# Two decode layers on one core: the second form of the layers behind a branch as two nested loops, its watch tiles placed behind the load places, and the register load moved ahead of the last norm

## The chip, the cores and the metric

The kernel runs on one core of a Trainium2 chip. A core has five engines, each with an instruction stream of its own: TensorE (PE, matrix products; its weight loads are listed as PEld), VectorE (DVE), ScalarE (ACT), GpSimd (POOL) and SyncE (SP), which here starts nearly all DMA transfers. The engines wait for each other through semaphores. Data lies in HBM, in SBUF (128 partitions, addressed by byte within a partition) and in PSUM, where matrix products are summed. The metric is the device time of one execution in microseconds (us), lower is better.

## The reference

Two attention blocks and two MLP blocks in turn, for a batch of 8 with one new position each (x is 8 x 448). Attention has 16 query heads over 8 key-value heads of width 256 with a cache of 4096 positions; both attention blocks use the same cache and weights, and so do both MLP blocks.

```python
def _A_ref(x, k_cache, v_cache, wq, wo):
    q = (x @ wq) ...                                   # 8 x 16 heads x 256
    scores = einsum("bhqd,bhkd->bhqk", q, k) * (Dh ** -0.5)
    p = softmax(scores, axis=-1)
    o = einsum("bhqk,bhkd->bhqd", p, v)
    return o ... @ wo
def _B_ref(x, w1, w2, w3, w4):
    ...                                                # for one position hs is zero
    x1 = x + hs
    return x1 + gelu(layernorm(x1) @ w3) @ w4
x = x + _A_ref(layernorm(x), ...)
x = x + _B_ref(layernorm(x), ...)
x = x + _A_ref(layernorm(x), ...)
x = x + _B_ref(layernorm(x), ...)
```

The key and value caches are 8 x 8 x 4096 x 256 bf16 each, 134 MB each. The softmax of the reference takes off the largest score; a softmax without that gives the same numbers as long as the exponentials neither overflow nor vanish.

## The kernel before

The kernel holds the layers in two forms. The first, `layers_unshifted`, is the fast one: its softmax takes the exponential of the scores as they are. Beside the work it keeps a watch: `seen` gathers sums and reciprocals of the softmax denominators (POOL adds them at L574). Near the end (L1338 to L1343) PE and DVE boil `seen` down to one number, and DVE writes 0 or 1 into `bad`. The second form, `layers_shifted`, computes the same layers again with the maximum taken off, slowly. It runs only if `bad` is 1: every engine loads `bad` into a register (`values_load`, L39) and compares it at a branch (`tc.If`, L40). For the inputs of this case `bad` is 0, so the second form's instructions are not executed. They stand in each engine's program all the same, between the branch and the program's end. With the flag at 0 an engine runs a short else block, which brings its semaphores to the counts that the second form would have left, and then branches over the second form's instructions to the end (L1892 in the profile), where all engines meet at barriers. SP's else block waits first for the output transfers.

The fast form streams the caches. SBUF holds 17 places of 8 KB per partition in one tile, `places`; a K tile pair of 2 MB or a V chunk of 1 MB (in halves, 512 KB) lands in a place, is used, and the place is given to the next load. All loads are issued by SP in an order that a planner in the Python code writes out (`items`, `emit_loads`, `load_k` at L962, `load_v` at L976 and L979). K is transposed in place by DVE (L1054), PE makes the scores (L1069), ACT the exponentials (L1078), PE the products with V (L1137 and, for the last units, L1153). Some K and V chunks stay in SBUF or PSUM from the first attention block to the second. Projections, norms and MLP of each row run as generators, stepped between tiles. The scheduler of the framework is switched off for this part (`manual_schedule`): instructions stand in the order in which the code emits them.

After the last V chunk the last four rows are finished one operation after the other: DVE adds the attention's output to x (L1572), squares and sums (L1585, L1586, PE at L1588, DVE at L1590), centres (L1604), POOL takes the powers for the norm (L1614), PE multiplies with w3 (L1623), ACT applies gelu (L1656), PE multiplies with w4 (L1672), DVE adds (L1681), and SP and ACT send the output in two transfers each (L1683).

In SBUF the tiles are placed in the order of their pools. The pool `flags` with `seen` and `bad` is opened first, so these two lie at bytes 16512 and 16576, and `places` begins at byte 16608 of each partition.

The second form (`layers_shifted`, L1689 and on) is Python loops that are unrolled into the program: two layers, in each 8 rows x 8 key-value heads, and for each pair of row and head some 130 instructions on PE, 12 on DVE, two loads on SP. The register load in the profile's L39 stands where it is written, behind all of the fast form, though SP's was emitted ahead of its output transfers.

Of the kernel before, what the change touches and what calls it, by code (L numbers as in the profile page):

```python
# [8 lines left out]
FP32 = mybir.dt.float32  # L9
BF16 = mybir.dt.bfloat16  # L10
U32 = mybir.dt.uint32
ACT = mybir.ActivationFunctionType
ALU = mybir.AluOpType
# [5 lines left out]
def kernel(  # L19
# [15 lines left out]
    flags = ctx.enter_context(tc.tile_pool(name="flags", bufs=1))  # L35
    seen = flags.tile([128, 12], FP32, name="seen")
    bad = flags.tile([128, 1], mybir.dt.int32, name="bad")
    layers_unshifted(tc, seen[:], bad[:], A_x, A_k_cache, A_v_cache, A_wq, A_wo, B_x, B_w1, B_w2, B_w3, B_w4, out)
    flag = tc.nc.values_load(bad[0:1, 0:1], min_val=0, max_val=1)  # L39
# [5 lines left out]
def layers_unshifted(  # L45
    ctx: ExitStack,
    tc: tile.TileContext,
    seen: bass.AP,
    bad: bass.AP,
# [71 lines left out]

    nc.gpsimd.memset(seen, 0.0)
# [1443 lines left out]
    while gens:  # L1566
        step(10 * len(items))

# [113 lines left out]
    for q in range(4):  # L1682
        (nc.scalar if q % 2 else nc.sync).dma_start(  # L1683
            out[:, 0, W * q : W * q + W], xo[32 * q : 32 * q + Bn]
        )


@with_exitstack
def layers_shifted(  # L1689
# [44 lines left out]
    OT = keep.tile([128, Hq, 2, Bn], BF16, name="OT_s")  # L1734
# [38 lines left out]
    for _ in range(2):  # L1773
# [6 lines left out]
        for b in range(Bn):  # L1780
            for g in range(G):
                kt = work.tile([128, NS, Dh], BF16, name="kt")
                nc.sync.dma_start(kt[:], A_k_cache[b, g].rearrange("(p n) d -> p n d", p=128))
                vt = work.tile([128, NS, Dh], BF16, name="vt")
                nc.sync.dma_start(vt[:], A_v_cache[b, g].rearrange("(p n) d -> p n d", p=128))
                q_ps = psum.tile([128, 2, Dh], FP32, name="q_ps")
                nc.tensor.matmul(
                    q_ps[:].rearrange("p h d -> p (h d)"),
                    identb[:Bn, b : b + 1].to_broadcast([Bn, 128]),
                    q[:, 2 * Dh * g : 2 * Dh * (g + 1)],  # L1790
# [3 lines left out]
                q_all = work.tile([128, 2, Dh], FP32, name="q_all")  # L1794
                nc.vector.tensor_scalar_mul(q_all[:], q_ps[:], float(Dh) ** -0.5)
                s = work.tile([128, 2, NS], FP32, name="s")
                top = work.tile([128, 2], FP32, name="top")
                for h in range(2):
                    prod = work.tile([128, NS, Dh], FP32, name="prod")
                    nc.vector.tensor_tensor(  # L1800
                        prod[:],
                        kt[:],
                        q_all[:, h].unsqueeze(1).to_broadcast([128, NS, Dh]),
                        ALU.mult,
                    )
                    nc.vector.tensor_reduce(s[:, h], prod[:], mybir.AxisListType.X, ALU.add)
                nc.vector.tensor_reduce(top[:], s[:], mybir.AxisListType.X, ALU.max)
                top_ps = psum.tile([2, 128], FP32, name="top_ps")
                nc.tensor.matmul(top_ps[:], top[:], ident[:], start=True, stop=True)
                most = work.tile([2, 1], FP32, name="most")  # L1810
                nc.vector.tensor_reduce(most[:], top_ps[:], mybir.AxisListType.X, ALU.max)
                all_ps = psum.tile([128, 2], FP32, name="all_ps")
                nc.tensor.matmul(
                    all_ps[:], most[:].to_broadcast([2, 128]), ident[:2, :2], start=True, stop=True
                )
                down = work.tile([128, 2], FP32, name="down")
                nc.vector.tensor_scalar_mul(down[:], all_ps[:], -1.0)
                p = work.tile([128, 2, NS], FP32, name="p")
                z = work.tile([128, 2], FP32, name="z")
                for h in range(2):  # L1820
                    nc.scalar.activation(
                        p[:, h],
                        s[:, h],
                        ACT.Exp,
                        bias=down[:, h : h + 1],
                        accum_out=z[:, h : h + 1],
                    )
                z_ps = psum.tile([128, 2], FP32, name="z_ps")
                nc.tensor.matmul(z_ps[:], ones[:], z[:], start=True, stop=True)
                rz = work.tile([128, 2], FP32, name="rz")  # L1830
                nc.vector.reciprocal(rz[:], z_ps[:])
                pb = work.tile([128, NS, 2], BF16, name="pb")
                for h in range(2):
                    nc.vector.tensor_scalar(
                        pb[:, :, h], p[:, h], rz[:, h : h + 1], 1.0, ALU.mult, ALU.mult
                    )
                o_ps = psum.tile([128, 2, 2], FP32, name="o_ps")
                for j in range(2):
                    for n in range(NS):
                        nc.tensor.matmul(  # L1840
# [56 lines left out]
```

## Time and profile before

| what | value |
|---|---|
| median of 3 runs | 1039.92 us (1039.06 to 1040.02) |
| the profiled execution | 1039.2 us |
| its span, first to last instruction | 1037.4 us |
| instructions executed | 28804 |
| PE / PEld busy | 660.3 / 417.4 us (64% / 40%) |
| DVE / ACT / POOL busy | 585.7 / 213.3 / 35.4 us (56% / 21% / 3%) |
| granted TensorE clock, mean | 0.639 |
| read from HBM | 419.63 MB, 405 GB/s over the span |

The profile is one execution, recorded by the hardware. Times are in us from the first instruction, durations of single instructions in ns. L12 is line 12 of the kernel before. An engine's name with a q (SPq, PEldq) is its instruction sequencer: register loads, branches, waits and DMA issues are its work and are not counted as busy. `x2: 43/46/49, 1031.5 to 1033.2` reads: two of these, shortest, median and longest duration, and the start of the first and of the last. A row by stretch gives the stretch and its length, then PE, PEld, DVE, ACT and POOL busy in us with the number of instructions, the granted clock, the busy share of the 16 DMA engines and GB/s. A row of DMA queues gives packets, MB and the time that the packets took as a share of 16 engines over the span; a queue of kind "instruction" carries the engines' programs. The chain that ended last is followed back from the last instruction, and its shares say in whose work the span went.

### The profile page before, as it was taken

The numbers are of one execution on the slowest core, as the hardware profiler recorded it, in microseconds if no ns is written. First come the engines' busy times: TensorE is split into PE (matmuls) and PEld (weight loads), VectorE is DVE, ScalarE is ACT, GpSimd is POOL, SyncE is SP. The second block draws the span as 40 slices with busy tenths as digits, with TensorE's granted clock in tenths as the row PEclk, the third lists the DMA queues.
The fourth block names the chain that finished last, engine by engine and source line by source line (L and its number), as shares of the span: only waits on it lengthen the run. The fifth ranks groups of instructions, "written<-read, shape, count | busy, mean of one in ns | idle before, by whom it ended". The sixth has DMA issues, their size and how long they took to land.

```text
span 1037.4 us, 28804 instructions
## 1 busy us (share of the span) xinstructions
PE 660.3 (64%) x12708; PEld 417.4 (40%) x12708; DVE 585.7 (56%) x1213; ACT 213.3 (21%) x689; POOL 35.4 (3%) x138
## 2 busy tenths in 40 slices
PE   2164445875587657765874687557765875686674
PEld 2032223553255334533552355334432453355454
DVE  6345576259616951695159615961696169625661
ACT  1010111141214121312141214121411141214110
POOL 0000000000000000000000000000000000000100
PEclk9999555576556556655566666565655566656555
DMA  9999999999999999999999999999999999999993
GB/s 381 410 425 420 420 423 415 399 423 423 412 400 425 425 409 391 414 424 411 402 417 425 411 403 420 424 412 392 424 422 406 402 417 423 411 392 414 419 419 148
DMA packets 68020, 421.58 MB, mean 406 GB/s; under 512 B 7080, under 2 KB 11952, under 8 KB 42288
## 3 DMA queue, kind: packets, MB, share of 16 engines
q1 hardware_dynamic: 67840, 419.66, 98.7%
q8 instruction: 101, 1.65, 0.6%
q14 instruction: 31, 0.25, 0.1%
q10 hardware_dynamic: 48, 0.01, 0.0%
HBM read 419.63 MB, written 0.01 MB: 405 GB/s over the span
## 4 chain that ended last, share of the span: by engine, by line
DMA 48%; DVE 24%; PE 20%; issue 4%; ACT 2%; SPq 1%; POOL 0%; DVEq 0%; ACTq 0%; POOLq 0%
DMA places<-in_A_v_cache_dram 36%; DVE places L1054 18%; DMA places<-in_A_k_cache_dram 11%; PE sc L1069 8%; PE o L1137 5%; PE misc L634 2%; PE misc L205 2%; DVE store L1100 2%; DVE qbd L449 1%; DMA w_sb<-in_B_w_dram 1%; PE misc L566 1%; SPq L224 1%; ACT p_n L1078 1%; PE misc L487 1%; DVE rz L569 1%
## 5 line engine op out<-in xcount | busy, mean ns | idle before, releaser
L1054 DVE STREAM_TRANSPOSE places<-places 128x512 uint32<-128x512 uint32 (+2 forms) x384 | 443.8, 1212 | 44.4 <-DMA places<-in_A_k_cache_dram 43.9
L1137 PE MATMUL o<-places,ptw 128*8 128x256 bf16 x3808 | 245.9, 382 | 139.6 <-DMA places<-in_A_v_cache_dram 110.5
L1069 PE MATMUL sc<-places,qbd 128*8 128x256 bf16 (+1 forms) x4736 | 237.1, 355 | 149.3 <-DVE places L1054 147.9
L1069 PEld LDWEIGHTS <-qbd 128*8 128x8 bf16 x4736 | 123.2, 104 | 218.6 <-DVE places L1054 125.3
L1137 PEld LDWEIGHTS <-ptw 128*8 128x8 bf16 x3968 | 102.5, 101 | 205.1 <-issue 127.4
L1078 ACT ACTIVATE p_n<-sc 128x256 bf16<-128x256 f32 x128 | 95.6, 747 | 329.4 <-PE sc L1069 326.8
L1319 ACT COPY ptw<-psv 128x32 bf16<-128x32 bf16 x248 | 52.7, 228 | 180.0 <-PE o L1137 178.4
L449 DVE CAST qbd<-misc 32x16 bf16<-32x16 f32 (+1 forms) x184 | 30.8, 167 | 63.6 <-PE misc L443 61.8
L634 PE MATMUL misc<-R_t,o_t 128*128 128x4 f32 (+1 forms) x212 | 45.6, 321 | 28.0 <-DVE qbd L449 11.6
L634 PEld LDWEIGHTS misc<-R_t,o_t 128*128 128x128 f32 x212 | 41.4, 272 | 44.4 <-issue 17.8
L569 DVE RECIPROCAL rz<-misc 128x4 f32<-128x4 f32 (+1 forms) x55 | 9.5, 172 | 84.9 <-PE misc L566 40.4
L1127 ACT CAST psv<-misc 128x128 bf16<-128x128 f32 x64 | 17.0, 266 | 195.7 <-PE misc L1120 195.7
L1105 ACT COPY places<-store 128x1024 bf16<-128x1024 bf16 x40 | 40.3, 1029 | 10.5 <-PE o L1137 10.1
L566 PE MATMUL misc<-zm,few 128*128 128x4 f32 (+1 forms) x110 | 28.6, 331 | 19.2 <-DVE zm L558 16.8
L574 POOL TENSOR_TENSOR seen<-seen,rz 128x4 f32<-128x4 f32 (+1 forms) x55 | 11.1, 202 | 842.2 <-DVE rz L569 813.1
L566 PEld LDWEIGHTS misc<-zm,few 128*128 128x128 f32 x110 | 23.8, 269 | 35.0 <-DVE zm L558 23.3
L1078 ACT ACTIVATION_READ_ACCUMULATOR p_n<-sc 128x1 f32 x128 | 34.1, 266 | 0.0
L205 PEld LDWEIGHTS <-w_sb 128*128 128x128 bf16 x896 | 27.4, 104 | 16.1 <-issue 16.1
L588 ACT COPY o_t<-o 128x256 f32<-128x256 f32 x53 | 19.8, 373 | 57.7 <-PE o L1137 57.7
L1100 DVE TENSOR_SCALAR store<-places 128x512 uint32<-128x512 uint32 x40 | 24.8, 674 | 0.0
L1120 PEld LDWEIGHTS <-p_n 128*128 128x128 bf16 x256 | 11.6, 105 | 29.9 <-issue 18.9
L638 DVE CAST qT<-misc 128x8 bf16<-128x8 f32 (+1 forms) x37 | 7.3, 196 | 27.9 <-PE misc L634 20.2
(165 smaller groups left out, 394.0 us busy)
## 6 DMA issues: line engine op xcount, KB each, us to landing
places<-in_A_k_cache_dram SPq DMA_DIRECT2D x79, 2048.0 KB, 15.3
places<-in_A_v_cache_dram SPq DMA_DIRECT2D x193, 512.0 KB, 7.1
places<-in_A_v_cache_dram SPq DMA_DIRECT2D x87, 1024.0 KB, 19.1
places<-in_A_k_cache_dram SPq DMA_DIRECT2D x34, 1024.0 KB, 11.8
rest<-in_A_v_cache_dram SPq DMA_DIRECT2D x8, 640.0 KB, 16.8
places<-in_A_wq_dram SPq DMA_DIRECT2D x5, 768.0 KB, 13.1
places<-in_A_v_cache_dram SPq DMA_DIRECT2D x8, 384.0 KB, 16.3
wo_sb<-in_A_wo_dram SPq DMA_DIRECT2D x1, 2688.0 KB, 19.0
```

Source lines behind the costliest of these rows:

```text
L205: nc.tensor.matmul(bass.AP(out.tensor, out.offset, [out.ap[0], (1, WIDE)]), w, x.to_broadcast([128, WIDE]), start=start, stop=stop, skip_g ...
L449: nc.vector.tensor_copy(qbd[32 * a : 32 * a + 32, :, g0 : g0 + ng, a, :], qs.rearrange("p e (f g u h) -> p (e f) u g h", f=2, u=2, h=2)[:, ...
L566: nc.tensor.matmul(z_ps, ones, zm[:], start=True, stop=True)
L569: nc.vector.reciprocal(rz[:], z_ps)
L634: nc.tensor.matmul(ot_ps[:, j], o_sb[:].rearrange("p (i j) -> p j i", j=2)[:, j], R, start=True, stop=True)
L1054: nc.vector.transpose(w, w)
L1069: nc.tensor.matmul(sc[32 * k : 32 * k + 8, 128 * (x % 2) : 128 * (x % 2 + nx)], qbd[:, ep, gp % 2].rearrange("p a h -> p (a h)"), v, start ...
L1078: nc.scalar.activation(p_sb[:, :, :, 2 * u : 2 * u + 2].rearrange("p t i x -> p x t i"), sc[:, 0:256].rearrange("p (x t i) -> p x t i", x= ...
L1100: nc.vector.tensor_single_scalar(kept_words.bitcast(U32), words.bitcast(U32), 0, op=ALU.bitwise_or)
L1105: nc.scalar.copy(words, kept_words.bitcast(BF16))
L1137: nc.tensor.matmul(o_ps[32 * q : 32 * q + 8, :], ptz[:, at : at + 8], v[:, y * Dh : (y + 1) * Dh] if v2 is None or y < PR else v2[:, (y - ...
L1319: nc.scalar.copy(ptw[:, ring_of[it], :, 6:8], psv[slot_of[it[0]]][:, it[2]])
```

## The change

Three things change. First, in the second form the loop over the two layers and the loop over the 64 pairs of row and head become loops of the engines (`tc.For_i`), so that each body stands in the program once. For that the second form is rewritten in part: queries go through a DRAM tile `q_rows` and are broadcast by a DMA, the loads take their row from the loop's register, probabilities stay unscaled in bf16 and the output is scaled, turned by PE, and stored at a register's offset. Second, `seen` and `bad` are no longer a pool of their own ahead of the others but tiles of the pool `consts`, asked for after the tile `places`; `places` then begins at byte 16512. Third, the register load of `bad` is moved from the outermost function into `layers_unshifted`, behind the last tile and ahead of the last norm, and its check of the loaded value against its bounds is left out. In the built program the fast form's instructions are otherwise the same, in the same order.

```diff
--- before.py
+++ after.py
@@ -32,11 +32,7 @@
     out: bass.AP,
 ):
 
-    flags = ctx.enter_context(tc.tile_pool(name="flags", bufs=1))
-    seen = flags.tile([128, 12], FP32, name="seen")
-    bad = flags.tile([128, 1], mybir.dt.int32, name="bad")
-    layers_unshifted(tc, seen[:], bad[:], A_x, A_k_cache, A_v_cache, A_wq, A_wo, B_x, B_w1, B_w2, B_w3, B_w4, out)
-    flag = tc.nc.values_load(bad[0:1, 0:1], min_val=0, max_val=1)
+    flag = layers_unshifted(tc, A_x, A_k_cache, A_v_cache, A_wq, A_wo, B_x, B_w1, B_w2, B_w3, B_w4, out)
     with tc.If(flag > 0, preferred_fallthrough_block=False):
         layers_shifted(tc, A_x, A_k_cache, A_v_cache, A_wq, A_wo, B_x, B_w1, B_w2, B_w3, B_w4, out)
 
@@ -45,8 +41,6 @@
 def layers_unshifted(
     ctx: ExitStack,
     tc: tile.TileContext,
-    seen: bass.AP,
-    bad: bass.AP,
     A_x: bass.AP,
     A_k_cache: bass.AP,
     A_v_cache: bass.AP,
@@ -119,6 +113,8 @@
         n_few[0] += n
         return few[:, at : at + n]
 
+    seen = consts.tile([128, 12], FP32, name="seen")[:]
+    bad = consts.tile([128, 1], mybir.dt.int32, name="bad")[:]
     nc.gpsimd.memset(seen, 0.0)
     usel = small(4)
     for u in range(2):
@@ -1565,6 +1561,12 @@
         step(idx, it in narrow)
     while gens:
         step(10 * len(items))
+    flag = nc.values_load(
+        bad[0:1, 0:1],
+        min_val=0,
+        max_val=1,
+        skip_runtime_bounds_check_because="a comparison writes 0 or 1",
+    )
 
 
     nb = Bn - MID
@@ -1683,6 +1685,7 @@
         (nc.scalar if q % 2 else nc.sync).dma_start(
             out[:, 0, W * q : W * q + W], xo[32 * q : 32 * q + Bn]
         )
+    return flag
 
 
 @with_exitstack
@@ -1731,7 +1734,11 @@
     nc.sync.dma_start(rows[:], A_x.rearrange("b s d -> (b s) d"))
     x = keep.tile([Bn, D], FP32, name="x_s")
     nc.vector.tensor_copy(x[:], rows[:])
-    OT = keep.tile([128, Hq, 2, Bn], BF16, name="OT_s")
+    OT = keep.tile([128, Bn * G, 2, 2], BF16, name="OT_s")
+    dram = ctx.enter_context(tc.tile_pool(name="q_rows", bufs=1, space=bass.MemoryType.DRAM))
+    q_rows = dram.tile([Bn * G, 2 * Dh], BF16, name="q_rows")
+    k_all = A_k_cache.rearrange("b g (p n) d -> (b g) p n d", p=128)
+    v_all = A_v_cache.rearrange("b g (p n) d -> (b g) p n d", p=128)
 
     def norm(dst, src):
         mean = work.tile([Bn, 1], FP32, name="mean")
@@ -1770,84 +1777,83 @@
             )
         return ps[:, 0:width]
 
-    for _ in range(2):
+    with tc.For_i(0, 2, 1):
         xn = work.tile([Bn, D], BF16, name="xn")
         norm(xn[:], x[:])
         xT = columns(xn, 112, KC, "xT_s")
         q = work.tile([Bn, HD], BF16, name="q_s")
         for at in range(0, HD, 512):
             nc.vector.tensor_copy(q[:, at : at + 512], times(xT, wq, KC, at, 512))
-        for b in range(Bn):
-            for g in range(G):
-                kt = work.tile([128, NS, Dh], BF16, name="kt")
-                nc.sync.dma_start(kt[:], A_k_cache[b, g].rearrange("(p n) d -> p n d", p=128))
-                vt = work.tile([128, NS, Dh], BF16, name="vt")
-                nc.sync.dma_start(vt[:], A_v_cache[b, g].rearrange("(p n) d -> p n d", p=128))
-                q_ps = psum.tile([128, 2, Dh], FP32, name="q_ps")
+        nc.sync.dma_start(q_rows[:].rearrange("(b g) c -> b (g c)", b=Bn), q[:])
+        with tc.For_i(0, Bn * G, 1) as i:
+            kt = work.tile([128, NS, Dh], BF16, name="kt")
+            nc.sync.dma_start(kt[:].unsqueeze(1), k_all[bass.ds(i, 1)].rearrange("o p n d -> p o n d"))
+            vt = work.tile([128, NS, Dh], BF16, name="vt")
+            nc.sync.dma_start(vt[:].unsqueeze(1), v_all[bass.ds(i, 1)].rearrange("o p n d -> p o n d"))
+            qb = work.tile([128, 2, Dh], BF16, name="qb")
+            nc.sync.dma_start(
+                qb[:].rearrange("p h d -> p (h d)"),
+                q_rows[bass.ds(i, 1), :].to_broadcast([128, 2 * Dh]),
+            )
+            q_all = work.tile([128, 2, Dh], FP32, name="q_all")
+            nc.vector.tensor_scalar_mul(q_all[:], qb[:], float(Dh) ** -0.5)
+            s = work.tile([128, 2, NS], FP32, name="s")
+            top = work.tile([128, 2], FP32, name="top")
+            for h in range(2):
+                prod = work.tile([128, NS, Dh], FP32, name="prod")
+                nc.vector.tensor_tensor(
+                    prod[:],
+                    kt[:],
+                    q_all[:, h].unsqueeze(1).to_broadcast([128, NS, Dh]),
+                    ALU.mult,
+                )
+                nc.vector.tensor_reduce(s[:, h], prod[:], mybir.AxisListType.X, ALU.add)
+            nc.vector.tensor_reduce(top[:], s[:], mybir.AxisListType.X, ALU.max)
+            top_ps = psum.tile([2, 128], FP32, name="top_ps")
+            nc.tensor.matmul(top_ps[:], top[:], ident[:], start=True, stop=True)
+            most = work.tile([2, 1], FP32, name="most")
+            nc.vector.tensor_reduce(most[:], top_ps[:], mybir.AxisListType.X, ALU.max)
+            all_ps = psum.tile([128, 2], FP32, name="all_ps")
+            nc.tensor.matmul(
+                all_ps[:], most[:].to_broadcast([2, 128]), ident[:2, :2], start=True, stop=True
+            )
+            down = work.tile([128, 2], FP32, name="down")
+            nc.vector.tensor_scalar_mul(down[:], all_ps[:], -1.0)
+            p = work.tile([128, NS, 2], BF16, name="p")
+            z = work.tile([128, 2], FP32, name="z")
+            for h in range(2):
+                nc.scalar.activation(
+                    p[:, :, h],
+                    s[:, h],
+                    ACT.Exp,
+                    bias=down[:, h : h + 1],
+                    accum_out=z[:, h : h + 1],
+                )
+            z_ps = psum.tile([2, 1], FP32, name="z_ps")
+            nc.tensor.matmul(z_ps[:], z[:], ones[:, 0:1], start=True, stop=True)
+            rz = work.tile([2, 1], FP32, name="rz")
+            nc.vector.reciprocal(rz[:], z_ps[:])
+            o_ps = psum.tile([2, Dh], FP32, name="o_ps")
+            for n in range(NS):
                 nc.tensor.matmul(
-                    q_ps[:].rearrange("p h d -> p (h d)"),
-                    identb[:Bn, b : b + 1].to_broadcast([Bn, 128]),
-                    q[:, 2 * Dh * g : 2 * Dh * (g + 1)],
+                    o_ps[:], p[:, n], vt[:, n], start=(n == 0), stop=(n == NS - 1)
+                )
+            o_row = work.tile([2, Dh], BF16, name="o_row")
+            nc.vector.tensor_scalar(o_row[:], o_ps[:], rz[:], 1.0, ALU.mult, ALU.mult)
+            turn = psum.tile([128, 2, 2], FP32, name="o_turn")
+            for j in range(2):
+                nc.tensor.matmul(
+                    turn[:, j],
+                    o_row[:, 128 * j : 128 * j + 128],
+                    identb[:2, :2],
                     start=True,
                     stop=True,
                 )
-                q_all = work.tile([128, 2, Dh], FP32, name="q_all")
-                nc.vector.tensor_scalar_mul(q_all[:], q_ps[:], float(Dh) ** -0.5)
-                s = work.tile([128, 2, NS], FP32, name="s")
-                top = work.tile([128, 2], FP32, name="top")
-                for h in range(2):
-                    prod = work.tile([128, NS, Dh], FP32, name="prod")
-                    nc.vector.tensor_tensor(
-                        prod[:],
-                        kt[:],
-                        q_all[:, h].unsqueeze(1).to_broadcast([128, NS, Dh]),
-                        ALU.mult,
-                    )
-                    nc.vector.tensor_reduce(s[:, h], prod[:], mybir.AxisListType.X, ALU.add)
-                nc.vector.tensor_reduce(top[:], s[:], mybir.AxisListType.X, ALU.max)
-                top_ps = psum.tile([2, 128], FP32, name="top_ps")
-                nc.tensor.matmul(top_ps[:], top[:], ident[:], start=True, stop=True)
-                most = work.tile([2, 1], FP32, name="most")
-                nc.vector.tensor_reduce(most[:], top_ps[:], mybir.AxisListType.X, ALU.max)
-                all_ps = psum.tile([128, 2], FP32, name="all_ps")
-                nc.tensor.matmul(
-                    all_ps[:], most[:].to_broadcast([2, 128]), ident[:2, :2], start=True, stop=True
-                )
-                down = work.tile([128, 2], FP32, name="down")
-                nc.vector.tensor_scalar_mul(down[:], all_ps[:], -1.0)
-                p = work.tile([128, 2, NS], FP32, name="p")
-                z = work.tile([128, 2], FP32, name="z")
-                for h in range(2):
-                    nc.scalar.activation(
-                        p[:, h],
-                        s[:, h],
-                        ACT.Exp,
-                        bias=down[:, h : h + 1],
-                        accum_out=z[:, h : h + 1],
-                    )
-                z_ps = psum.tile([128, 2], FP32, name="z_ps")
-                nc.tensor.matmul(z_ps[:], ones[:], z[:], start=True, stop=True)
-                rz = work.tile([128, 2], FP32, name="rz")
-                nc.vector.reciprocal(rz[:], z_ps[:])
-                pb = work.tile([128, NS, 2], BF16, name="pb")
-                for h in range(2):
-                    nc.vector.tensor_scalar(
-                        pb[:, :, h], p[:, h], rz[:, h : h + 1], 1.0, ALU.mult, ALU.mult
-                    )
-                o_ps = psum.tile([128, 2, 2], FP32, name="o_ps")
-                for j in range(2):
-                    for n in range(NS):
-                        nc.tensor.matmul(
-                            o_ps[:, j],
-                            vt[:, n, 128 * j : 128 * j + 128],
-                            pb[:, n],
-                            start=(n == 0),
-                            stop=(n == NS - 1),
-                        )
-                nc.vector.tensor_copy(
-                    OT[:, 2 * g : 2 * g + 2, :, b], o_ps[:].rearrange("p j h -> p h j")
-                )
-        o_cols = OT[:].rearrange("p h j b -> p (h j) b")
+            nc.vector.tensor_copy(
+                OT[:, bass.ds(i, 1)].rearrange("p o h j -> p (o h) j"),
+                turn[:].rearrange("p j h -> p h j"),
+            )
+        o_cols = OT[:].rearrange("p (b g) h j -> p (g h j) b", b=Bn)
         nc.vector.tensor_add(x[:], x[:], times(o_cols, wo, HD // 128, 0, D))
         n1 = work.tile([Bn, D], FP32, name="n1")
         norm(n1[:], x[:])
```

## Prediction

> **What bounds the kernel now.** I read the page first (DMA queues, chain that ended last), then busy time by stretch, then by line the instructions of the register load (L39), the branch (L40) and the program's end (L1892).
>
> From the page:
>
> ```profile
> q1 hardware_dynamic: 67840, 419.66, 98.7%
> q8 instruction: 101, 1.65, 0.6%
> q14 instruction: 31, 0.25, 0.1%
> ...
> DMA 48%; DVE 24%; PE 20%; issue 4%; ACT 2%; SPq 1%; POOL 0%; DVEq 0%; ACTq 0%; POOLq 0%
> ```
>
> The load queue is busy for 98.7% of the span, so until the last load lands nothing but the transfers counts. Queues 8 and 14 carry instructions: the engines fetch their programs while they run. Busy time by stretch:
>
> ```profile
> 1005.00:1023.00 18.00, 12.66 (x335) 11.04 (x336) 2.41 (x18) 2.67 (x6) 0.68 (x4) 0.50 0.88 357
> 1023.00:1037.40 14.40, 5.46 (x160) 4.59 (x159) 3.47 (x21) 0.53 (x3) 1.99 (x2) 0.50 0.03 7
> ```
>
> After 1023 us the DMA share is 0.03: the last 14.4 us are a serial tail, in which a microsecond is a microsecond. The output DMAs, the branch, and what stands behind it:
>
> ```profile
> L1683 SPq DMA_DIRECT2D out_dram<-places x2: 287/330/373, 1030.7 to 1031.1; - x2
> ```
>
> ```profile
> L40 POOLq COMPARE_BRANCH  x2: 38/42/45, 1027.8 to 1029.3; - x2
> L40 PEldq COMPARE_BRANCH  x2: 95/1836/3577, 1030.2 to 1030.6; - x2
> L40 DVEq COMPARE_BRANCH  x2: 51/53/55, 1031.1 to 1031.3; - x2
> L40 SPq COMPARE_BRANCH  x2: 43/46/49, 1031.5 to 1033.2; - x2
> L40 ACTq COMPARE_BRANCH  x2: 38/46/53, 1032.1 to 1032.2; - x2
> ```
>
> ```profile
> L1892 SPq EVENT_SEMAPHORE  x10: 17/28/28, 1036.1 to 1037.3; - x10
> ...
> L1892 POOLq DRAIN  x3: 34/41/82, 1029.4 to 1037.1; - x3
> ...
> L1892 PEldq DRAIN  x2: 8/40/73, 1034.2 to 1037.0; - x2
> L1892 DVEq DRAIN  x2: 10/34/57, 1034.2 to 1036.9; - x2
> L1892 ACTq DRAIN  x2: 8/38/67, 1034.9 to 1036.9; - x2
> ```
>
> Each engine branches twice: once on the flag, once from the short else block over the second form's code to the end. POOL needs 0.16 us for the second (branch 1029.29, next instruction 1029.45). The others need PE 3.6 us (1030.56 to 1034.20), DVE 2.9 (1031.29 to 1034.25), ACT 2.6 (1032.23 to 1034.87), SP 2.85 (1033.23 to 1036.08). In each such gap the trace's packet records have one instruction packet about 1.1 us after the branch (DVE 1032.35, ACT 1033.18, SP 1034.44 of 8192 B; PE 1031.66 of 16384 B), and a second some 0.6 us after the engine goes on. POOL has none. So a far jump costs a fetch of the target's page. SP is last: it branches only when the output has landed (its waits end at 1033.2), so its 2.85 us end the kernel.
>
> **The change, part by part.** *1. The second form becomes loops.* The data does not take the branch (its work is not in the trace), so only the size of the code jumped over matters. Counted in the two built programs, by engine, before and after: PE 17619 and 355 (364 with the second passes of three fp32 products), DVE 1910 and 126, SP 522 and 89, ACT 275 and 61, POOL 21 and 62. The fast path is the same instructions in the same order but for part 3, and the else block and the end have as many as before.
>
> Which pages does an engine hold? One instruction is 64 B, so a packet is 128 instructions, for PE 256; PE's 101 packets against its 25,520 executed instructions say one packet per page walked, and the pair after a jump (target, then next) says that page and next are held. Aligning packet times with instruction counts, SP stands about 54 into its page at the jump: 74 are left there and 128 in the next, and 89 lands 15 into the held next page. ACT: about 10 + 128 left, jump 61, held. DVE: about 12 + 128, jump 126, held by some 14, near the edge. POOL stays in its own. PE: about 79 + 256 = 335 left, jump 364: beyond.
>
> Sum: SP goes on at 1033.23 + 0.16 (POOL's row) = 1033.39 instead of 1036.08. Its eight waits and drain took 0.63 us (1036.08 to 1036.71): 1034.02. PE is late next: it still fetches, branches no earlier (its branch waits for its own last matmul), drains at 1034.20 with 0.07, and POOL's gathering then stands at about 1034.31 instead of 1036.71: **-2.40 us**. Were PE's page held, SP would end it: 1036.71 - 1034.02 = -2.69. DVE, if it fetches after all, comes at 1034.25, no later than PE. The ends: 0 (a target in the next page stalls like a far one, nearest row SP's 2.85) and -2.7. I take -2.4, since the page count puts three engines inside and PE outside.
>
> [...]
>
> *2. The watch's two tiles lie behind the places.* `places` starts at byte 16512 of each partition instead of 16608 (32 past a multiple of 64 before, 0 after). No instruction changes; the target addresses of about 51,000 packets of 4, 8 and 16 KB do, 3,190 per engine. Rows: 1792-byte packets take 74 ns at best, both into `wo_sb` (a multiple of 64) and into `places`; 4096-byte ones 159 ns mostly into `wq_sb` (aligned) and, early, into `places`. So alignment shows no price: 0. Ends: V's 8192-byte packets mostly take 313 ns but 309 when alone, K's 614 against 611, V's 4096 about half at 162 or more against 159. If the shift gave all that back, (15,488 x 4 + 10,112 x 3 + 12,700 x 3) / 16 engines = 8.1 us gained; I know no row against the mirror image, so +6.4 us (2 ns each) is the other end.
>
> *3. Register loads ahead of the last norm.* Each engine waits for `bad` (written 1022.79, 0.155 us), loads (0.479 to 0.562 us), and goes on.
>
> ```profile
> L39 SPq TENSOR_LOAD <-bad x1: 479/479/479, 1023.0 to 1023.0; - x1
> ...
> L39 POOLq TENSOR_LOAD <-bad x1: 498/498/498, 1027.2 to 1027.2; - x1
> L39 PEldq TENSOR_LOAD <-bad x1: 488/488/488, 1029.6 to 1029.6; - x1
> L39 DVEq TENSOR_LOAD <-bad x1: 545/545/545, 1030.5 to 1030.5; - x1
> L39 ACTq TENSOR_LOAD <-bad x1: 562/562/562, 1031.4 to 1031.4; - x1
> ```
>
> What is removed lies on no path that ends: DVE's, PE's and ACT's stood in front of branches whose engines come in before SP. What is added queues in front of the norm. DVE: behind L581 (ends 1024.17), ahead of L1572, which starts at 1024.81 when PE's L487 is done: 1024.17 + 0.545 + 0.07 = 1024.79, just hidden. PE: behind L487 (last ends 1024.77), ahead of L1588's wait for DVE (over at 1025.43): 1024.77 + 0.488 + 0.10 = 1025.36, hidden. ACT has nothing between 1022.6 and 1028.6, POOL nothing from 1018.5 to 1027.2. SP's load stays where it was; its range check (0.2 us at 1023.5) goes while SP waits for the output until 1030.7: 0. If DVE's cover failed, up to +0.6 us; in the queue order it could gain nothing. I take 0.
>
> *4. Two register moves on SP* ahead of the first barrier: 0.035 us each by POOL's move at 0.73; SP reaches that barrier 0.3 us before PE: 0.
>
> The profiled execution took 1039.2 us, span 1037.4, 1.8 outside. With -2.4 the span is 1035.0 and that execution 1036.8. The median of the runs is 1039.92, 0.7 above it; on the median: 1039.9 - 2.4 = **1037.5**.
>
> **Rivals.**
> *PE's target is held too.* For: only its two packets after the jump tell its depth, and 29 instructions decide. Against: the same two packets. SP ends it: 1037.2. [...]
> *The next page does not help.* A taken branch refetches unless it stays in its page, as POOL's did, the only short jump in the trace. SP then stalls 2.85 us as before: 1039.9. Against: the next page has been fetched long before (SP's last packet at 944.5).
> *The shift speeds the loads.* 1039.9 - 2.4 - 8.1 = 1029.4 at the full end, 1033.5 at half. Against: equal best times on both alignments. [...]
> *Slower: the shift slows the loads.* Same place, other sign: each nanosecond on 3,190 packets an engine is 3.2 us, so it eats the gain at 0.75 ns and is slower by 0.2% from 1.4 ns. At 2 ns: 1039.9 - 2.4 + 6.4 = 1043.9. For: the queue is full, nothing hides it. Against: the same best times.
>
> **How the numbers follow.** Forecast 0.45 (1037.5), PE held 0.20 (1037.2), no help from the next page 0.17 (1039.9), loads faster 0.10, loads slower 0.08. A measurement of this kernel can tell about 0.2% (2.1 us; the three runs span 1.0). The forecast clears that by 0.3 us, so three in four of it count as faster, nine in ten of the second case, all of the fourth: 0.34 + 0.18 + 0.10 = 0.62 faster; 0.30 within; 0.08 slower. The range leaves out the last two cases (0.18): from 1036.0 (second case, less 1.2 for run to run and the 1.8 us outside the span) to 1040.4 (third case plus 0.5). The first case alone: 1036.7 to 1038.3.
>
> **What would show it.** SP's first L1892 instruction within 0.3 us of its second branch; no instruction packet between; PE's second branch still about 3.6 us long and its drain the last to come in; DVE's L1572 and PE's L1588 no later after the last load; medians of 8192- and 16384-byte packets unchanged at 313 and 614 ns. It is wrong if SP still shows a gap near 2.9 us, if the 98.7% stretch ends at another time by over 1 us, or if L1572 waits for the load.

## The result, and the profile after

The changed kernel takes 1034.18 us (median of 6 runs, 1034.10 to 1035.51), the kernel before beside it 1040.08 us (6 runs, 1039.06 to 1041.33): a ratio of 0.9944, 95% interval 0.9931 to 0.9957. That is faster by 0.56%. The forecast was 1037.5 us with a range down to 1036.0: the sign was right, the size was not, and the time lies below the range.

The profiled execution took 1034.15 us, its span 1032.4 (before: 1039.2 and 1037.4). The rows that answer to those of before follow. From the page, the queues (packets, MB, share), what was read from HBM, and the chain:

```profile
q1 hardware_dynamic: 67840, 419.66, 99.0%
q8 instruction: 101, 1.65, 0.7%
q14 instruction: 28, 0.23, 0.1%
...
HBM read 419.63 MB, written 0.01 MB: 406 GB/s over the span
...
DMA 47%; DVE 26%; PE 18%; issue 4%; ACT 2%; SPq 1%; POOL 0%; DVEq 0%; ACTq 0%
```

The same packets and bytes, and still a queue that is full all the time. But the span is shorter, so the same packets took less time each. Three instruction packets are gone from queue 14 (31 to 28): the page fetches of SP, DVE and ACT behind the branch.

The first operation behind the last load (L1572 before, L1574 now), and busy time by stretch, as in the prediction:

```profile
L1572 DVE TENSOR_TENSOR xT<-xT,store x1: 172/172/172, 1024.8 to 1024.8; 128x16 f32<-128x16 f32 x1
L1574 DVE TENSOR_TENSOR xT<-xT,store x1: 171/171/171, 1021.3 to 1021.3; 128x16 f32<-128x16 f32 x1
```

```profile
1000.00:1019.40 19.40, 12.43 (x351) 11.05 (x340) 4.01 (x21) 3.05 (x7) 0.68 (x4) 0.66 0.90 371
1019.40:1032.40 13.00, 5.55 (x160) 4.68 (x160) 3.58 (x22) 0.53 (x3) 1.99 (x2) 0.50 0.03 6
```

This splits the gain in two. The add starts at 1021.30 us instead of 1024.81: **the stretch of the loads is 3.51 us shorter**. From there to the end it is 11.08 us instead of 12.60: **the tail is 1.52 us shorter**. Together 5.03 us of span. The prediction had 0 for the first and 2.40 for the second.

In the tail, the register loads, the output's issues, the branches and the end:

```profile
L1564 SPq TENSOR_LOAD <-bad x1: 478/478/478, 1019.6 to 1019.6; - x1
L1564 ACTq TENSOR_LOAD <-bad x1: 475/475/475, 1019.6 to 1019.6; - x1
...
L1564 DVEq TENSOR_LOAD <-bad x1: 541/541/541, 1020.4 to 1020.4; - x1
L1564 PEldq TENSOR_LOAD <-bad x1: 488/488/488, 1020.8 to 1020.8; - x1
```

```profile
L1685 SPq DMA_DIRECT2D out_dram<-places x2: 298/332/367, 1027.2 to 1027.6; - x2
```

```profile
L36 POOLq COMPARE_BRANCH  x2: 38/42/45, 1023.7 to 1025.8; - x2
L36 PEldq COMPARE_BRANCH  x2: 95/1984/3872, 1026.1 to 1027.0; - x2
L36 DVEq COMPARE_BRANCH  x2: 51/53/55, 1026.9 to 1027.3; - x2
L36 SPq COMPARE_BRANCH  x2: 43/46/49, 1028.0 to 1030.6; - x2
L36 ACTq COMPARE_BRANCH  x2: 38/44/49, 1028.1 to 1028.3; - x2
```

```profile
L1898 SPq EVENT_SEMAPHORE  x10: 17/28/28, 1031.1 to 1032.3; - x10
...
L1898 DVEq DRAIN  x2: 10/34/57, 1027.9 to 1031.9; - x2
L1898 ACTq DRAIN  x2: 8/44/79, 1028.7 to 1031.9; - x2
L1898 PEldq DRAIN  x2: 8/40/73, 1031.0 to 1032.0; - x2
```

SP branches the second time at 1030.56 and goes on at 1031.06: 0.50 us where it was 2.85. DVE needs 0.56 (2.96 before), ACT 0.45 (2.64), POOL 0.16 as before; PE still 3.93. The loads are hidden: the output transfers are issued 5.92 us behind the add in both kernels. What is new is how late SP sees its output. Its waits for the output ended 2.08 us behind the first issue before, now 2.93 us (at 1030.14 of 1027.21): 0.85 us of the gain in the gap is lost again.

### The profile page after: what moved, and what is told of

Same layout as the page of the kernel before. It is cut to its first block, busy times and chain, and to the rows that moved or that the text cites. A ratio compares the mean times of both kernels' runs of the same rounds, so it can differ in the third digit from the quotient of the medians.

```text
span 1032.4 us, 28804 instructions
## 1 busy us (share of the span) xinstructions
PE 659.1 (64%) x12708; PEld 418.1 (41%) x12708; DVE 585.6 (57%) x1213; ACT 213.1 (21%) x689; POOL 35.4 (3%) x138
## 4 chain that ended last, share of the span: by engine, by line
DMA 47%; DVE 26%; PE 18%; issue 4%; ACT 2%; SPq 1%; POOL 0%; DVEq 0%; ACTq 0%
DMA places<-in_A_v_cache_dram 29%; DVE places L1050 21%; DMA places<-in_A_k_cache_dram 17%; PE sc L1065 7%; PE o L1133 5%; PE misc L201 2%; PE misc L630 2%; DVE store L1096 1%; ACT p_n L1074 1%; DMA w_sb<-in_B_w_dram 1%; DVE qbd L445 1%; SPq L220 1%; PE misc L483 1%; PE misc L562 1%; PE misc L1116 0%
## 5 line engine op out<-in xcount | busy, mean ns | idle before, releaser
L1050 DVE STREAM_TRANSPOSE places<-places 128x512 uint32<-128x512 uint32 (+2 forms) x384 | 443.8, 1212 | 42.7 <-DMA places<-in_A_k_cache_dram 42.5
L570 POOL TENSOR_TENSOR seen<-seen,rz 128x4 f32<-128x4 f32 (+1 forms) x55 | 11.1, 202 | 838.6 <-DVE rz L565 807.9
## 6 DMA issues: line engine op xcount, KB each, us to landing
places<-in_A_v_cache_dram SPq DMA_DIRECT2D x8, 384.0 KB, 14.7
```

The lines of the kernel that those rows point to most:

```text
L1050: nc.vector.transpose(w, w)
```

## The experiments

The stretch to the add and the tail behind it are read separately in each run; times are of the profiled execution, medians of all runs.

**Where the loads start in SBUF.** Two kernels take the place of the tiles apart from the rest of the change, then four move the start of `places` by moving small tiles of the pool `consts` ahead of it. The first is the kernel before, with only the start changed (16576); the second is the changed kernel with the watch tiles ahead of the places again (16608).

```diff
 a_base_only (from the kernel before)
-    seen = flags.tile([128, 12], FP32, name="seen")
-    bad = flags.tile([128, 1], mybir.dt.int32, name="bad")
+    both = flags.tile([128, 16], FP32, name="both")
+    seen = both[:, 0:12]
+    bad = both[:, 12:13].bitcast(mybir.dt.int32)
 c_watch_ahead (from the changed kernel)
+    seen = consts.tile([128, 12], FP32, name="seen")[:]
+    bad = consts.tile([128, 1], mybir.dt.int32, name="bad")[:]
     places_t = consts.tile([128, NC * PB], BF16, name="places")
...
-    seen = consts.tile([128, 12], FP32, name="seen")[:]
-    bad = consts.tile([128, 1], mybir.dt.int32, name="bad")[:]
```

Expected of a_base_only:

> The kernel before with seen and bad in one tile of 64 bytes ahead of the places: places start at byte 16576 (0 past a multiple of 64, 192 past one of 256) instead of 16608 (32 and 224); the second form unrolled and the register load late as before. Theory 64 (what counts is whether packets start on a multiple of 64 bytes): the stream gains its whole 3.5 us, the tail nothing, so about 1036.5 and L1572's counterpart near 1021.3. [...] Theory elsewhere (the stream's gain came with the smaller program, not with the address): no change, 1040.

Expected of c_watch_ahead:

> The changed kernel with seen and bad again ahead of the places (start 16608): loops and early register load stay. [...] Theory elsewhere: the stream keeps its gain, about 1034.2.

c_watch_ahead took 1038.11 us (12 runs; ratio 0.9985, 0.9976 to 0.9993), its add came at 1024.75 us, nearly where it had been before (1024.81), and its tail stayed short (11.38). So 3.45 of the 3.51 us hang on the place of the two tiles. The page of c_watch_ahead has before's rate again:

```profile
HBM read 419.63 MB, written 0.01 MB: 405 GB/s over the span
```

a_base_only took 1039.34 us (12 runs, 1037.05 to 1041.18; ratio 0.9994, 0.9983 to 1.0005): no measurable gain from 16576. It is not clean: it moved every tile in SBUF by 32 bytes, which takes `wq_sb` and `wo_sb` off a multiple of 256 on which they lay, and its profiled execution, with the add at 1023.14, is the fastest of its runs. Its tail is 12.12 us against 12.60 before, with nothing in the tail changed: differences of up to 0.5 us between single tails can be chance.

The other kernels differ from the changed one only in which of the small tiles `few`, `fold`, `low`, `seen` and `xq` are asked for ahead of `places`; `rest`, which lies right behind `places`, moves with it, and the tiles behind stay where they are. For the first:

```diff
 s_base16640 (from the changed kernel)
     PB = 16 * Dh
+    few = consts.tile([128, 16], FP32, name="few")
+    fold = consts.tile([128, 8], FP32, name="fold")
+    low = consts.tile([128, 2, 4], FP32, name="low")
     places_t = consts.tile([128, NC * PB], BF16, name="places")
```

s_base16544 moves `fold` alone, s_base16672 also `xq` and s_base16704 also `seen`. Expected of s_base16640:

> The changed kernel with few, fold and low ahead of the places: start 16640, a multiple of 64 and of 256. Theory 64: as the changed kernel, 1034.2 within 0.5. [...]

Expected of s_base16544:

> The changed kernel with fold ahead of the places: start 16544, 32 past a multiple of 64 and 160 past one of 256. So far the starts 224, 192, 128 and 0 past a multiple of 256 gave the last add to x at 1024.8, 1023.1, 1021.3 and 1010.1 us. [...] Theory 64 (a start off 64 costs more than one on it): as 224, 1024.8, about 1038.

Expected of s_base16672:

> The changed kernel with few, fold, low and xq ahead of the places: start 16672, 32 past a multiple of 256. [...]

Expected of s_base16704:

> The changed kernel with few, fold, low and seen ahead of the places: start 16704, 64 past a multiple of 256 and a multiple of 64. [...]

Measured, in order of the start's distance past a multiple of 256 bytes; the last three columns are the share of 4, 8 and 16 KB packets that took no more than the best time (159, 309 and 611 ns), counted in the packet records:

| start | past 256 | kernel | median us | ratio, 95% | add at us | 4 KB | 8 KB | 16 KB |
|---|---|---|---|---|---|---|---|---|
| 16640 | 0 | s_base16640 | 1023.05 | 0.9841 (0.9826 to 0.9856) | 1010.10 | 98% | 99% | 97% |
| 16672 | 32 | s_base16672 | 1038.31 | 0.9980 (0.9970 to 0.9989) | 1024.88 | 35% | 14% | 11% |
| 16704 | 64 | s_base16704 | 1036.04 | 0.9963 (0.9952 to 0.9973) | 1022.34 | 41% | 16% | 18% |
| 16512 | 128 | the changed kernel | 1034.18 | 0.9944 (0.9931 to 0.9957) | 1021.30 | 54% | 37% | 37% |
| 16544 | 160 | s_base16544 | 1035.07 | 0.9955 (0.9937 to 0.9972) | 1021.50 | 48% | 22% | 25% |
| 16608 | 224 | c_watch_ahead | 1038.11 | 0.9985 (0.9976 to 0.9993) | 1024.75 | 36% | 12% | 9% |

The page of s_base16640:

```profile
span 1021.2 us, 28804 instructions
...
q1 hardware_dynamic: 67840, 419.66, 99.1%
...
HBM read 419.63 MB, written 0.01 MB: 411 GB/s over the span
...
L1050 DVE STREAM_TRANSPOSE places<-places 128x512 uint32<-128x512 uint32 (+2 forms) x384 | 443.5, 1213 | 38.9 <-DMA places<-in_A_k_cache_dram 38.7
```

The same bytes, 411 GB/s where it was 406, and the transposes on the moved tile as long as in the changed kernel (1213 and 1212 ns): the start acts on the transfers, not on the engines that read the tile. With the start on a multiple of 256 nearly every packet takes its best time, and the packets' time, over 16 engines, sums to 1011.7 us on the load queue (1021.8 at 16512, 1024.3 before). The two neighbours that move the same three tiles and one more (16672, 16704) lose the gain, so it is not those tiles' own place. The cost falls with the distance to the nearest multiple of 256: 32 bytes to either side is worst (16672, 16608), then 64, 96 (16544), 128; and 0 is far the best. The shares keep this order; the medians of neighbours among 64, 96 and 128 lie within each other's intervals. a_base_only (16576, 64 below the boundary) has shares of 42%, 15% and 14%, near those of 16704 (64 above); why its median gained so little stays open. A cost that grows with the bytes past the boundary would have put 16672 (add at 1024.88 us) next to 16640 (1010.10), and multiples of 64 would have put 16704 (1022.34) there: both fall. What makes a packet off the boundary slower was not shown.

All six starts lie within 128 bytes of 16640, so they alone do not show that every multiple of 256 does as well. Packets of 1792 bytes (7 x 256) speak for it. `wo_sb` and `w4_sb` start at multiples of 256 in these six kernels and in the kernel before (190464 and 211968), and their 2304 packets of this size (told by their time, 34 to 50 us) all took the best time, 74 ns, in each of these seven traces. In a_base_only, which put these tiles 32 bytes below, 18% did.

**The target page of PE.** Sixty tiny products on PE early in the stream (they ran at 54 us) shift its code by 120 instructions, a weight load and a product each, so that the jump of 364 should end in the page next to the branch's.

```diff
 p_page60 (from the changed kernel)
+        if idx == 10:
+            for _ in range(60):
+                nc.tensor.matmul(
+                    store[4][:, 0:8], identb[:], identb[:, 0:8], start=True, stop=True
+                )
```

Expected of p_page60:

> The changed kernel with 60 small matrix products more (120 instructions of PE) while PE idles at 32 us, their results unused: the branch moves from about 177 to about 41 into its page of 256, so the target, 364 on, falls into the next page. Page theory: PE's second branch takes 0.5 us as the other engines' do, instead of 3.9, and PE's packet behind it is gone; SP is last as before, so 1034.1 within 0.4. Rival (a jump of that length fetches anyway): PE's branch stays at 3.9. If PE's packet were what holds up the output: SP's waits end 0.9 us sooner, 1033.3.

1034.35 us (4 runs; ratio 0.9946, 0.9925 to 0.9967), tail 11.15 us. PE's branch in the trace of p_page60:

```profile
L36 PEldq COMPARE_BRANCH  x2: 95/1208/2322, 1025.9 to 1026.8; - x2
```

PE needs 2.38 us (1026.82 to 1029.20) instead of 3.93: neither the 0.5 expected nor the rival's 3.9. One 16 KB packet had started at 1026.74, ahead of the branch, and ended at 1027.66; there is none for the target by itself. So a target in the next page brings no fetch of its own for PE either, and one in a page behind that does; that PE waited for the page already on order is read from these times. The end does not move, since SP comes last in either case. SP's waits for the output still end 2.99 us behind the first issue (2.93 in the changed kernel), so it is not PE's packet behind its branch that holds up the output.

**The register loads back at the end.** The loads of `bad` are written behind the output transfers again; d_late_load does this to the changed kernel, b_base_late to s_base16640, and b_base_late_page adds the sixty products of p_page60.

```diff
 d_late_load, b_base_late
-    flag = nc.values_load(
-        bad[0:1, 0:1],
...
             out[:, 0, W * q : W * q + W], xo[32 * q : 32 * q + Bn]
         )
+    flag = nc.values_load(
+        bad[0:1, 0:1],
...
     return flag
```

Expected of d_late_load:

> The changed kernel with the register load behind the output transfers. My step 3 (the load's place costs and gains nothing): 1034.2 within 0.4. Rival (the early load takes work out of the tail and is part of the 1.5 us): up to 0.6 us slower, 1034.8, by one load of 0.48 to 0.56 us.

Expected of b_base_late:

> Start 16640 as in the run with 1023.05, and the register load behind the output transfers on every engine. The late load shortened the tail from 11.08 to 10.20 us at start 16512; if that holds here, the tail is 10.2 and the time 1022.2. Rival (that gain was chance): 11.1 and 1023.05.

Expected of b_base_late_page:

> The same with the 60 small products on PE, which bring PE's next page in before its branch. With the late load PE drains at 1030.74, 0.1 us behind SP's 1030.64, so PE is last by a little: PE's branch 2.4 us instead of 3.6, SP last, 0.15 us less than the run without: 1022.0. Rival (the pages of PE do not matter): the same as without.

The tails are 10.20, 10.04 and 9.95 us, against 11.08 in both kernels with the early loads. In d_late_load SP's waits for the output end 1.84 us behind the first issue instead of 2.93, and PE (goes on at 1030.74), not SP (1030.02 and its eight waits), is now last:

```profile
L36 PEldq COMPARE_BRANCH  x2: 95/1838/3581, 1026.8 to 1027.1; - x2
L36 DVEq COMPARE_BRANCH  x2: 51/53/55, 1027.6 to 1027.8; - x2
...
L36 SPq COMPARE_BRANCH  x2: 43/46/49, 1028.7 to 1029.5; - x2
```

So the early loads cost the tail 0.9 to 1.0 us, behind the output's issue. All traces agree: the waits end 2.92 to 3.28 us behind the first issue in the ten kernels with early loads other than f_dve_pad (below), and 1.80 to 2.08 in the five with late ones. In the medians: d_late_load 1033.66 (ratio 0.9940, 0.9927 to 0.9953), which cannot be told from the changed kernel's 1034.18; b_base_late **1021.88 us** (5 runs; ratio 0.9823, 0.9806 to 0.9840), the fastest median of all, 1.2 us ahead of s_base16640, a difference that their intervals leave open; b_base_late_page 1022.25 (0.9827, 0.9811 to 0.9842), so the products change nothing measurable.

**Which engine's branch delays the output.** With the early loads, one of the output's last eight packets starts 0.3 to 0.5 us behind the seven others (in the changed kernel at 1028.90, the others by 1028.59), and it starts as an instruction packet of 8192 B ends (1028.47 + 0.42 = 1028.89). One of the eight packets sent just ahead of them is late in the same way (1028.88, the others by 1028.43). The instruction packet starts 1.15 us behind DVE's second branch. An early load lets DVE branch 0.11 us behind the first output issue; with the late one it is 0.56 us. A first pair of kernels was to delay the branch of one engine with a second register load there:

> Start 16640, early load on all engines, and one load more on DVE alone, behind the output transfers: it puts off DVE's branch by some 0.55 us and changes nothing else. DVE theory (with the early load DVE reaches its branch while the output is under way, and its next instruction page, 8 KB, lands on the DMA engine of one output packet): the last output packet comes within 0.1 us of the others, SP's waits end about 2.0 us after the first output DMA instead of 2.9, time 1022.2. ACT theory (ACT's first output DMA takes 0.54 us instead of 0.31 with the early load, and that is what is late): no change, 1023.05.

> The same with the extra load on ACT alone. DVE theory: no change, 1023.05, the last output packet still right behind an instruction packet. ACT theory: SP's waits end 0.9 us sooner, 1022.2.

The second load's result was not used, and neither trace has a second load, only one semaphore instruction more; DVE branched 0.11 us behind the first issue as before. So both in effect repeat s_base16640 (1022.96 and 1022.62 us, 5 runs each; tails 11.07) and decide nothing. The second pair puts three small operations on one engine behind the output transfers:

```diff
 f_dve_pad, f_act_pad (from s_base16640)
+    pad = temp(W)
+    for _ in range(3):
+        nc.vector.tensor_add(pad, x_out, pad if _ else x_norm)            # f_dve_pad
+        nc.scalar.activation(pad, pad if _ else x_out, ACT.Identity)      # f_act_pad
     return flag
```

Expected of f_dve_pad:

> The changed kernel with the places at 16640 (register loads ahead of the norm), and three small adds of 128x112 on DVE between the last add of the output and the branch; their result is not used. One such add took 0.27 us in the trace (274 ns), so DVE comes to its branch about 0.8 us later. In that kernel DVE branched 0.11 us behind the first output transfer's issue, its next page's packet (8192 B) started 1.15 us behind the branch, and the last of the 16 output packets started 0.37 us behind the seven others of its pair, as that packet ended. If it is DVE's page that delays the output: the page's packet now starts 2.0 to 2.1 us behind the first issue, when the output has gone; the last output packet starts within 0.05 us of the seven others, SP's waits for its output end 2.0 to 2.6 us behind the first issue instead of 2.93, and the stretch from the last add to x to the end is 10.2 to 10.8 us instead of 11.08; time 1022.1 to 1023.1. If it is ACT's page, or the early loads by themselves (ACT's first output issue takes 0.54 us with them and 0.31 without): the last output packet stays 0.35 us behind, the waits end at +2.93, the stretch is 11.0 to 11.1 us.

Expected of f_act_pad:

> The same kernel, with three small copies of 128x112 on ACT between its two output transfers' issues and its branch instead, their result not used: ACT branches 0.5 to 1 us later, DVE when it did. If it is DVE's page that delays the output, nothing changes: the last output packet starts 0.35 us behind the seven others, SP's waits end 2.93 us behind the first issue, the stretch to the end is 11.0 to 11.1 us. If it is ACT's page, the last output packet is level, the waits end at +1.9 to +2.6 and the stretch is 10.0 to 10.8 us.

The branches in the trace of f_dve_pad:

```profile
L36 DVEq COMPARE_BRANCH  x2: 51/53/55, 1016.1 to 1016.5; - x2
L36 SPq COMPARE_BRANCH  x2: 43/46/49, 1016.3 to 1018.0; - x2
L36 ACTq COMPARE_BRANCH  x2: 38/44/49, 1016.5 to 1016.6; - x2
```

and in that of f_act_pad:

```profile
L36 DVEq COMPARE_BRANCH  x2: 51/53/55, 1014.9 to 1015.3; - x2
L36 SPq COMPARE_BRANCH  x2: 43/46/49, 1016.0 to 1018.8; - x2
L36 ACTq COMPARE_BRANCH  x2: 38/44/49, 1016.8 to 1017.2; - x2
```

With DVE's branch 0.80 us later (0.91 behind the first output issue at 1015.57) all eight last output packets start within 0.06 us, SP's waits end 2.00 us behind the issue, and the tail is 10.15 us, though DVE does more. With ACT's branch later instead (1017.18), DVE's page starts at 1016.46 for 0.58 us, the last output packet follows at 1017.06, 0.48 behind the others, the waits end at 3.19 us and the tail is 11.34. It is DVE's branch. The times (1022.02 and 1022.48 us, two runs each) are too few to tell these two apart. The packet records do not name the DMA engine, so that the output packet stood behind the page on the same one is read from the times; in c_watch_ahead and s_base16704 the page's record starts 0.3 us after the first late packet's neighbours, and what held that packet until then is not seen. Nor is the late start the whole delay: the output's last packet ends 1.71 us behind the first issue in the changed kernel and 1.32 in d_late_load, 0.39 apart, while SP's waits are 1.09 apart (2.93 and 1.84). The rest lies between the packet's end and the wait's, and why stays open. Why ACT's first output issue takes 0.54 us with the early loads and 0.31 with the late ones stays open; with f_dve_pad it still did, and the tail was within 0.11 us of b_base_late's.

## Why the prediction was wrong

*Step 1, the loops: right in each engine, 0.34 us too good.* SP, DVE and ACT land in a page that they hold and PE does not, as the count of instructions said, DVE's narrow case included. That count took 64 B for an instruction; the trace of before gives 64.8 (PE's 101 packets of 16384 B for its 25,520 executed instructions). The price of such a jump was taken from POOL's row (0.16 us), which stays inside its own page; into the held next page it is 0.45 to 0.56. SP's gap shrank by 2.35 us, not by the 2.69 that this price gave it. As predicted PE's branch was as long as before (3.93 us, 3.64 before), and it would have come last with its drain had SP seen the output when it did before; d_late_load shows that order. The rival "PE's target is held" does not fit: PE's jump of 364 instructions was fetched.

*Step 2, the watch behind the places: the step that failed.* It was taken as 0 between -8.1 and +6.4; it is -3.51 us, and this alone puts the time below the range. Two readings went astray. First, "alignment shows no price" compared best times, which exist at every start; the share of packets that reach them is what the start changes (8 KB: 15% before, 37% after, 99% at 16640). The trace of before held the price. Of its 1792-byte packets, 100% of the 2304 into `wo_sb` and `w4_sb` took the best time, but 29%, 50% and 37% of those in the three later loads of this size into `places` (512 packets each); at 16640 these are 99 to 100%. And "V's 8192-byte packets mostly take 313 ns but 309 when alone" was the price, put down to company: at 16640 they take 309 in company too. Second, it sorted the starts by multiples of 64 and so expected the whole price or none; the boundary that counts in these runs is 256 (add at 1010.10 us on it, 1021.30 to 1024.88 off it), on which `wo_sb` and `wq_sb` lay, and the move from 224 to 128 past it gives back about a quarter of what 0 does (3.51 of 14.7 us). The sign that was to catch it, medians of 313 and 614 ns, hardly moves either: 312 and 613 now. The rival "the shift speeds the loads" described what happened, though its full end of 8.1 was short of the 11.2 us that 16640 gives to the stream beside 16512 (14.7 beside before), and got a chance of 0.10. The price does not grow with the distance past the boundary: 32 past it is as slow as 224 past it (add at 1024.88 and 1024.75 us).

*Step 3, the early loads: hidden where predicted, and paid for elsewhere.* L1574 and the norm behind it are not later, and DVE's load ends just in time, as worked out. But 0 was the price of the instructions' own time. "What is removed lies on no path that ends" left out that a packet of instructions follows a branch (1.15 us behind DVE's), and that the output was on its way at that time. Earlier by 0.45 us, DVE's page collides with the output: +0.85 us at SP's waits. So the tail gained 1.52 us: 2.35 of the gap less 0.85, and 0.02 elsewhere.

*Step 4, two register moves on SP:* nothing is seen of them: 0, as taken.

*The sum:* -3.51 - 2.35 + 0.85 is -5.01, the span's -5.03. The forecast came within 0.9 us on the tail and missed the loads.

## What to carry to other kernels

In a kernel bound by its loads, look at the start of the load tiles within a partition: moving three small tiles so that it is a multiple of 256 bytes was worth 11.1 us of 1034 in the medians, more than the whole change. Judge a transfer by the share of its packets that reach the best time, in the stretch where the queue is full; a best time only shows what is possible. And in these traces a branch near the end of the kernel also brought a DMA (8192 B, 1.15 us behind DVE's branch): where it falls just ahead of the output transfers, a later branch can be the faster one (DVE's 0.80 us later: a tail of 10.15 us instead of 11.08).

## What was not expected of the hardware

- A start 32 bytes off a multiple of 256 costs a stream of 4 to 16 KB packets 1.5% (add to x at 1024.88 us against 1010.10), as much as one 224 bytes past it; 128 past costs 1.1%.
- A jump into the next page, already held, took 0.45 to 0.56 us (ACT and DVE in the changed kernel); inside the page 0.16 (POOL, before and after); into a page that is not held 2.6 to 4.1 (2.64 for ACT before, 3.93 for PE in the changed kernel); into one that is on order but not yet there 2.0 to 2.4 (PE in p_page60 and b_base_late_page).
- With DVE's instruction packet of 8 KB (0.30 to 0.58 us long) among the output's packets, one packet in each of the last two output transfers started only as it ended, 0.3 to 0.6 us behind its neighbours, and the waits for the output ended 0.85 to 1.2 us later.
